# Chunk widths of a fused FFT and MLP kernel: 376, 368, 384, 368, eight times 512 and 432 columns in place of the widths of the frequency classes

## The chip, the cores and the metric

The kernel runs on one core of one Trainium2 chip. The metric is the device time of one execution in microseconds (us). Before the change the median of three runs is 850.53 us (849.95 to 851.07). The engines are named as in the profile: PE is TensorE (PEld its weight loads), DVE is VectorE, ACT is ScalarE, POOL is GpSimd, SP is SyncE, which issues most of the DMAs.

## The reference

```python
X = np.fft.fft(x, axis=1)                # x: (4, 3008, 256)
X = np.fft.fft(X, axis=2)
x = X.real.astype(np.float32).reshape(12032, 256)
h = x @ w_in                             # w_in: (256, 2048)
g = h * (1.0 / (1.0 + np.exp(-h)))       # silu
return (g @ w_out).astype(np.float32)    # w_out: (2048, 256)
```

A two-dimensional FFT of four batches, of which only the real part is kept, is followed by an MLP with a silu between its two products. All of it is in float32.

## The kernel before, in words

**Frequencies and classes.** The sequence is transformed for 1506 frequencies per batch, and each stands for itself and for its mirror. They come in four classes (k = 0 to 3) of 376, 378, 376 and 376 frequencies (`CLASS`, L40), so the four batches have 16 classes (c = 4b + k). `operand(c)` folds the input with sums and differences on DVE, ACT and POOL, `transform(c)` (L339) multiplies the folded rows by cosine and sine tables on PE into two PSUM tiles `po` of the tag `pq`, and `spread(c)` (L384) brings the result into SBUF. The FFT over the 256 features is not done on the data: it is multiplied into `w_in` at the start, which gives `abh` and `abl`.

**Columns and chunks.** The frequencies of all batches stand behind one another as 6024 columns. The MLP works on chunks of columns: `CHUNKS` (L42) has their widths and `STARTS` their first columns. Before the change the first four chunks are the four classes of batch 0, then come eight chunks of 512 and one of 422. A chunk has three SBUF tiles, made by `chunk(j)` (L378): `uv` with the high parts (`uvh`) and the remainders (`uvl`) of the transform's two halves, and `ub`, one row of it repeated on 128 partitions. Each has three buffers.

**Spread.** `spread(c, po)` cuts the class at the chunk borders into `parts` (L390). For each part ACT copies the high halves (L414), and DVE subtracts them from the source to get the remainders (L426). The row for `ub` is read out by a DMA on SP that repeats it on 128 partitions (L421). For k = 1 the source is PSUM, so ACT first copies the row into a tile `row` (L418), one for each part, and the high halves take one copy for each of the two tiles. For the other k the source is the SBUF tile `wide`, and its row is read from there. `row` has the tag `half` of the pool `fold_p`, which has three buffers; the tag is shared with the `wf` tiles in which blocks of the weights are put together, with `q`, and with half of the output tiles `o`.

**Steps.** A step is a chunk j and a block f of 128 of the 2048 hidden features: 13 chunks of 16 steps. `first(c, f)` (L443) has six matmuls (L449 to L451: high and low parts of weights and data) into two `pq` tiles. `act` (L459) makes `p` with `ub` on DVE (L463), then `h` as p + q and p - q for a frequency and its mirror (L464, L465). ACT applies silu (L480) and copies the rounded `g` high part (L483). `rest` (L488) makes the remainder of `g` on DVE (L495), a step later. `second(c, f)` (L497) has twelve matmuls (L512, L513, L519) into four accumulators. It runs three steps behind `first` (`LAG`), and at the end of a chunk ACT copies the accumulators (L528) and SP writes them out (L529). So PE has 18 matmuls a step, each as wide as the chunk. PSUM has four `pq` tiles, so `first` of one step waits until DVE has read the tiles of two turns ago.

**Order.** The order is written out by hand in the loop at L838, and every engine takes its work in that order. In the loop `first` of a step stands ahead of `second` of the step three before. `turns` (L784) says in which step a class is transformed: class 1 in step 11 of chunk 0, class 2 in step 12 of chunk 1, class 3 in step 12 of chunk 2, class 4 in step 3 of chunk 3, and so on. For class 1 `spread` runs inside `act` of its step, between `h` and the silu (`between`, L469). `clear_wo` puts blocks 6 and 7 of w_out into two `half` buffers in step 10 of chunk 0, and `low_wo` gives them back in step 12.

Of the kernel before, what the change touches and what calls it, by code (L numbers as in the profile page):

```python
# [38 lines left out]
NT = B * NC  # L39
CLASS = ((0, 376), (376, 378), (754, 376), (1130, 376))  # L40
CH = 512
CHUNKS = [n for _, n in CLASS] + [CH] * 8 + [422]  # L42
STARTS = [sum(CHUNKS[:j]) for j in range(len(CHUNKS))]
LAST = len(CHUNKS) - 1
LAG = 3
# [5 lines left out]
def fft_mlp(ctx, tc, x1, x2, x2_first, w_in, w_out, te_f, te_r, to_f, to_r, tz_r, t2_f, t2_r, t2f, rot1, rot2, dft, minus_eye, out):  # L51
# [326 lines left out]
    def chunk(j):  # L378
        if j not in chunks:
            uv = cp.tile([128, 2, 2, 512], F32R, tag="uv", name="uv")  # L380
            chunks[j] = uv[:, 0], uv[:, 1], cp.tile([128, 512], F32, tag="ub", name="ub"), CHUNKS[j], STARTS[j]
        return chunks[j]

    def spread(c, po):  # L384
# [4 lines left out]
        parts = []  # L389
        for j, (at, m) in enumerate(zip(STARTS, CHUNKS)):  # L390
            lo, hi = max(o, at), min(o + n, at + m)
# [381 lines left out]

    steps = [(j, f) for j in range(len(CHUNKS)) for f in range(NF)]
    plan = {}
# [238 lines left out]
```

## Time and profile before

| | |
|---|---|
| median of 3 runs | 850.53 us (849.95 to 851.07) |
| the profiled execution | 850.67 us |
| its span, from the first to the last instruction | 848.9 us |
| instructions in the span | 11020 |
| ACT, share of the span busy | 60% |
| DMA, mean over the span | 61 GB/s |

The span is 1.8 us shorter than the time of its execution. PE's granted clock is 1.00 in all forty slices of the span. Matmuls overlap in the engine, so a matmul's own duration is longer than the distance from its start to the next one's start; the distance is what PE's work takes. Where a row shows several instructions merged, its second number runs from the first start to the last end. A bracket at the end of a row is the engine's idle time ahead of it and what ended it.

### The profile page before, as it was taken

The numbers are of one execution on the slowest core, as the hardware profiler recorded it, in microseconds if no ns is written. First come the engines' busy times: TensorE is split into PE (matmuls) and PEld (weight loads), VectorE is DVE, ScalarE is ACT, GpSimd is POOL, SyncE is SP. The second block draws the span as 40 slices with busy tenths as digits, with TensorE's granted clock in tenths as the row PEclk, the third lists the DMA queues.
The fourth block names the chain that finished last, engine by engine and source line by source line (L and its number), as shares of the span: only waits on it lengthen the run. The fifth ranks groups of instructions, "written<-read, shape, count | busy, mean of one in ns | idle before, by whom it ended". The sixth has DMA issues, their size and how long they took to land.

```text
span 848.9 us, 11020 instructions
## 1 busy us (share of the span) xinstructions
PE 840.8 (99%) x4066; PEld 739.0 (87%) x4066; DVE 715.6 (84%) x1076; ACT 511.4 (60%) x650; POOL 166.3 (20%) x239
## 2 busy tenths in 40 slices
PE   8999999999999999999999999999999999999998
PEld 5799999999998888888888888888888888888997
DVE  5899999999898888998779988999787788777774
ACT  5767756556665565567566656467555655655554
POOL 4657550304040211304104000311000000000000
PEclk9999999999999999999999999999999999999999
DMA  9755454164250616116205201621020120120101
GB/s 319 275 141 73 107 103 73 21 93 63 9 138 0 109 51 94 17 9 149 10 1 148 8 3 51 107 10 50 0 10 1 50 10 0 51 10 0 50 1 42
DMA packets 24471, 52.12 MB, mean 61 GB/s; under 512 B 3633, under 2 KB 9265, under 8 KB 24417
## 3 DMA queue, kind: packets, MB, share of 16 engines
q1 hardware_dynamic: 20176, 38.21, 21.4%
q0 software_dynamic: 4240, 13.21, 8.6%
q8 instruction: 32, 0.52, 0.2%
q14 instruction: 23, 0.18, 0.1%
HBM read 36.17 MB, written 12.34 MB: 57 GB/s over the span
## 4 chain that ended last, share of the span: by engine, by line
PE 96%; DMA 2%; DVE 0%; ACT 0%; SPq 0%; issue 0%; ACTq 0%
PE acc L512 20%; PE acc L519 20%; PE acc L513 20%; PE pq L449 10%; PE pq L451 10%; PE pq L450 10%; PE pq L354 3%; DMA win<-in_w_in_dram 2%; PE pq L351 1%; PE acc L510 1%; PE pq L348 1%; ACT wf L82 0%; PE pq L682 0%; PE pw L589 0%; DVE wf L86 0%; SPq L78 0%
## 5 line engine op out<-in xcount | busy, mean ns | idle before, releaser
L480 ACT ACTIVATE h<-h 128x1024 f32<-128x1024 f32 (+4 forms) x208 | 202.6, 974 | 273.7 <-DVE h L465 271.2
L512 PE MATMUL acc<-g,woh 128*128 128x512 f32 (+3 forms) x824 | 305.7, 371 | 0.0
L513 PE MATMUL acc<-g,wol 128*128 128x512 f32 (+3 forms) x824 | 304.7, 370 | 0.0
L495 DVE TENSOR_TENSOR g<-h,g 128x1024 fp32r<-128x1024 f32 (+4 forms) x208 | 240.3, 1156 | 14.8 <-ACT g L483 14.6
L519 PE MATMUL acc<-g,woh 128*128 128x512 f32 (+3 forms) x824 | 211.3, 370 | 0.0
L483 ACT ACTIVATE g<-h 128x1024 fp32r<-128x1024 f32 (+4 forms) x208 | 202.5, 973 | 6.8 <-PE acc L513 0.5
L463 DVE SCALAR_TENSOR_TENSOR p<-ub,a,pq 128x512 f32<-128x512 f32 (+3 forms) x208 | 144.4, 694 | 67.9 <-PE pq L451 64.4
L512 PEld LDWEIGHTS acc<-g,woh 128*128 128x128 f32 x824 | 154.8, 188 | 21.0 <-ACT o L528 0.2
L513 PEld LDWEIGHTS acc<-g,wol 128*128 128x128 f32 x824 | 154.8, 188 | 20.2
L519 PEld LDWEIGHTS acc<-g,woh 128*128 128x128 f32 x824 | 152.1, 188 | 20.3
L449 PE MATMUL pq<-uv,abh 128*128 128x512 f32 (+3 forms) x416 | 156.9, 377 | 0.0
L451 PE MATMUL pq<-uv,abl 128*128 128x512 f32 (+3 forms) x416 | 154.1, 370 | 0.0
L450 PE MATMUL pq<-uv,abh 128*128 128x512 f32 (+3 forms) x416 | 153.9, 370 | 0.0
L464 DVE TENSOR_TENSOR h<-p,pq 128x512 f32<-128x512 f32 (+3 forms) x208 | 132.5, 637 | 21.7
L465 DVE TENSOR_TENSOR h<-p,pq 128x512 f32<-128x512 f32 (+3 forms) x208 | 131.1, 630 | 0.0
L449 PEld LDWEIGHTS pq<-uv,abh 128*128 128x128 f32 x416 | 78.3, 188 | 10.6 <-issue 0.2
L451 PEld LDWEIGHTS pq<-uv,abl 128*128 128x128 f32 x416 | 78.1, 188 | 10.2
L450 PEld LDWEIGHTS pq<-uv,abh 128*128 128x128 f32 x416 | 78.2, 188 | 10.1
L150 POOL DMA_DIRECT2D raw<-in_x_dram x22 | 19.1, 882 | 217.5 <-DMA raw<-in_x_dram 215.4
L234 POOL TENSOR_TENSOR ri<-ri,raw 128x256 f32<-128x256 f32 x24 | 22.8, 966 | 144.3 <-ACT ri L229 144.1
L528 ACT ACTIVATE o<-acc 128x512 f32<-128x512 f32 (+3 forms) x52 | 27.7, 556 | 14.4 <-PE acc L519 12.3
L218 POOL TENSOR_TENSOR raw<-raw 128x512 f32<-128x512 f32 x12 | 16.7, 1395 | 16.2 <-DMA raw<-in_x_dram 16.2
(140 smaller groups left out, 467.6 us busy)
## 6 DMA issues: line engine op xcount, KB each, us to landing
raw<-in_x_dram SPq DMA_DIRECT2D x22, 512.0 KB, 8.2
raw<-in_x_dram POOLq DMA_DIRECT2D x20, 512.0 KB, 7.8
out_dram<-o SPq DMA_DIRECT2D x32, 256.0 KB, 2.2
win<-in_w_in_dram SPq DMA_DIRECT2D x8, 512.0 KB, 8.8
wo<-in_w_out_dram SPq DMA_DIRECT2D x8, 512.0 KB, 9.6
out_dram<-o SPq DMA_DIRECT2D x12, 188.0 KB, 4.2
ub<-wide SPq DMA_DIRECT2D x6, 188.0 KB, 8.7
x_t<-in_x_first_dram SPq DMA_DIRECT2D x2, 512.0 KB, 9.8
```

The costliest lines, as they stand in the source:

```text
L449: nc.tensor.matmul(po, abh[:, i, fs], uvh[:, i, :n], start=True, stop=False)
L450: nc.tensor.matmul(po, abh[:, i, fs], uvl[:, i, :n], start=False, stop=False)
L451: nc.tensor.matmul(po, abl[:, i, fs], uvh[:, i, :n], start=False, stop=True)
L463: stt(p[:, :n], ub[:, :n], a128[f // 2][:, f % 2:f % 2 + 1], pq[0][:, :n], op0=ALU.mult, op1=ALU.add)
L464: tt(h[:, 0, :n], p[:, :n], pq[1][:, :n], op=ALU.add)
L465: tt(h[:, 1, :n], p[:, :n], pq[1][:, :n], op=ALU.subtract)
L480: nc.scalar.activation(h[:, sg, :n], h[:, sg, :n], AF.Silu)
L483: nc.scalar.activation(gh[:, sg, :n], h[:, sg, :n], AF.Copy)
L495: tt(gl[:, sg, :n], g[:, sg, :n], gh[:, sg, :n].bitcast(F32), op=ALU.subtract)
L512: nc.tensor.matmul(po, wo[0][f // 2][:, f % 2, es], gh[:, sg, :n], start=f == 0, stop=False)
L513: nc.tensor.matmul(po, wo[1][f // 2][:, f % 2, es], gh[:, sg, :n], start=False, stop=False)
L519: nc.tensor.matmul(accs[c][i][:, :n], wo[0][f // 2][:, f % 2, es], gl[:, sg, :n], start=False, stop=f == NF - 1)
```

## The change

One line changes. The widths of the first four chunks are no longer those of the classes, and the last chunk is 432 wide instead of 422. The sum is 6024 as before.

```diff
 CLASS = ((0, 376), (376, 378), (754, 376), (1130, 376))
 CH = 512
-CHUNKS = [n for _, n in CLASS] + [CH] * 8 + [422]
+CHUNKS = [376, 368, 384, 368] + [CH] * 8 + [432]
 STARTS = [sum(CHUNKS[:j]) for j in range(len(CHUNKS))]
 LAST = len(CHUNKS) - 1
```

The chunks now start at columns 0, 376, 744, 1128, 1496 and then every 512. Class 1 (columns 376 to 754) reaches into chunk 1 with 368 columns and into chunk 2 with 10; class 2 into chunk 2 with 374 and into chunk 3 with 2; class 3 into chunk 3 with 366 and into chunk 4 with 10. The classes of the other batches have as many parts as before, with borders ten columns further on. So `spread` issues three broadcasts more on SP, five instructions more on ACT and four more on DVE. PE has as many matmuls as before.

On ACT this is step 11 of chunk 0, from the end of step 10 (L483) over the spread of class 1 to the silu and the rounding of step 11. A line's bracket names the semaphores that the instruction waits for (DMAHW and a digit are the lanes of SP's DMAs, DMASW those of POOL's).

```order
 L483 ACTIVATE g<-h 128x2x376 [waits PE_49,Activation_49]
-L414 ACTIVATE uv<-pq_759 128x378 [waits PE_49]
-L414 ACTIVATE uv<-pq_760 128x378 [waits PE_49]
-L418 ACTIVATE row<-pq_760 1x378 [waits Pool_49]
+L414 ACTIVATE uv<-pq_759 128x368 [waits PE_49]
+L414 ACTIVATE uv<-pq_760 128x368 [waits PE_49]
+L414 ACTIVATE uv<-pq_759 128x10 [waits DMASW4_49,DMASW5_49,DMASW3_49,DMASW6_49,DMASW2_49,DMASW7_49,DMASW1_49,DMASW0_49]
+L414 ACTIVATE uv<-pq_760 128x10
+L418 ACTIVATE row<-pq_760 1x368 [waits Pool_49]
+L418 ACTIVATE row<-pq_760 1x10 [waits DMAHW6_49,Activation_49]
 L480 ACTIVATE h<-h 128x2x376 [waits DVE_49]
 L483 ACTIVATE g<-h 128x2x376 [waits Activation_49]
```

Two copies of ten columns and a second row copy have come in between the copies of the spread and the silu. The second row copy waits for a lane of SP's DMAs.

On DVE it is the same place, from the last `h` of step 11 (L465) to the remainder of `g` of step 10 (L495).

```order
 L465 TENSOR_TENSOR h<-p,pq_740 128x376
-L426 TENSOR_TENSOR uv<-pq_759,uv 128x378 [waits Activation_49]
-L426 TENSOR_TENSOR uv<-pq_760,uv 128x378 [waits PE_49,Activation_49]
+L426 TENSOR_TENSOR uv<-pq_759,uv 128x368 [waits PE_49,Activation_49]
+L426 TENSOR_TENSOR uv<-pq_760,uv 128x368 [waits PE_49,Activation_49]
+L426 TENSOR_TENSOR uv<-pq_759,uv 128x10 [waits DMASW7_49,DMASW0_49]
+L426 TENSOR_TENSOR uv<-pq_760,uv 128x10
 L495 TENSOR_TENSOR g<-h,g 128x2x376 [waits Pool_49]
```

Two remainders of ten columns have come in ahead of L495. The second wide remainder waits for ACT up to its last instruction of the spread, which was the only row copy before and is the second one now.

On SP this is the changed program there, from a load of w_out over the two broadcasts of class 1 to the next loads of x. A DMA waits until the lane that it takes has been left by its last user, and signals on that lane when it has landed.

```order
L78 DMA wo<-in_w_out_dram 128x2x1024 [waits DMAHW5_49,DMAHW1_49,DVE_49]
L421 DMA ub<-row 128x1x368 [waits DMAHW6_49,Activation_49]
L421 DMA ub<-row 128x1x10 [waits DMAHW7_49,Activation_49]
L145 DMA raw<-in_x_dram 128x1024 [waits DMAHW0_49,DMASW0_49,Pool_49]
L145 DMA raw<-in_x_dram 128x1024 [waits DMASW1_49,Pool_49]
```

The first broadcast takes lane 6 and the second, which is new, lane 7.

On PE this is `first` of step 13 of chunk 0, into the two PSUM tiles that the transform of class 1 had filled (pq_759 and pq_760; their buffers are pq_839 and pq_840 there before, pq_848 and pq_849 now).

```order
-L449 MATMUL pq_839<-uv,abh 128x376 [waits DVE_49]
-L450 MATMUL pq_839<-uv,abh 128x376
-L451 MATMUL pq_839<-uv,abl 128x376
-L449 MATMUL pq_840<-uv,abh 128x376 [waits DVE_49]
-L450 MATMUL pq_840<-uv,abh 128x376
-L451 MATMUL pq_840<-uv,abl 128x376
+L449 MATMUL pq_848<-uv,abh 128x376 [waits DVE_49,PE_49]
+L450 MATMUL pq_848<-uv,abh 128x376
+L451 MATMUL pq_848<-uv,abl 128x376
+L449 MATMUL pq_849<-uv,abh 128x376 [waits DVE_49,PE_49,Activation_49]
+L450 MATMUL pq_849<-uv,abh 128x376
+L451 MATMUL pq_849<-uv,abl 128x376
```

The matmuls stand where they stood; the first of each tile waits for DVE, which before meant the two wide remainders and now means the two of ten columns behind them, and the second tile also for ACT's last read of it, the second row copy.

## Rows read from the trace of the kernel before

**Rows 1.** The page, part 1: busy us, share of the span, instructions.

```profile
PE 840.8 (99%) x4066; PEld 739.0 (87%) x4066; DVE 715.6 (84%) x1076; ACT 511.4 (60%) x650; POOL 166.3 (20%) x239
```

**Rows 2.** The chain that ended last, in order of time: start us, us, what.

```profile
97.06 0.69 PE acc L519 x4
...
118.91 0.69 PE acc L519 x4
...
142.82 0.69 PE acc L519 x4
...
170.90 0.69 PE acc L519 x4
...
278.13 0.91 PE acc L519 x4
...
318.93 0.91 PE acc L519 x4
...
799.12 0.77 PE acc L519 x4
...
837.40 0.77 PE acc L519 x4
```

**Rows 3.** The waits: who waited for whom, us in total, times, longest.

```profile
PEld acc L512 <- ACT o L528: 0.2, 1, 0.2
```

**Rows 4.** ACT in order of time: start us, us, instruction [idle before].

```profile
66.39 0.49 ACT L414 ACTIVATE uv<-pq 128x378 fp32r<-128x378 f32 x1 [1.38 <-PE pq L354]
66.78 0.46 ACT L418 ACTIVATE row<-pq 1x378 f32<-1x378 f32 x1
67.14 0.81 ACT L480 ACTIVATE h<-h 128x752 f32<-128x752 f32 x1
```

**Rows 5.** SP's queue in order of time, 55 to 85 us.

```profile
67.26 0.52 SPq L421 DMA_DIRECT2D ub<-row  x1
80.90 2.88 SPq L145 DMA_DIRECT2D raw<-in_x_dram  x2
```

**Rows 6.** DMA issues by size: KB each, median us from issue to landing.

```profile
ub<-row SPq DMA_DIRECT2D x1, 189.0 KB, 8.7
...
ub<-wide SPq DMA_DIRECT2D x1, 135.0 KB, 7.0
...
ub<-row SPq DMA_DIRECT2D x1, 68.0 KB, 4.6
```

**Rows 7.** DVE in order of time, the spread of class 1.

```profile
67.27 0.55 DVE L426 TENSOR_TENSOR uv<-pq,uv 128x378 fp32r<-128x378 f32 x1 [1.42 <-ACT row L418]
67.74 1.21 DVE L495 TENSOR_TENSOR g<-h,g 128x752 fp32r<-128x752 f32 x1
```

**Rows 8.** PE in order of time, `first` of step 13 of chunk 0.

```profile
69.32 0.34 PE L449 MATMUL pq<-uv,abh 128*128 128x376 f32 x1
```

**Rows 9.** Groups by form, small copies and differences: busy us, mean ns, idle.

```profile
L292 ACT ACTIVATE sm<-sm 128x4 f32<-128x4 f32 x1 | 0.2, 184 | 0.0
...
L414 ACT ACTIVATE uv<-wide 128x60 fp32r<-128x60 f32 x1 | 0.3, 256 | 0.9 <-DVE wide L406 0.9
...
L313 DVE TENSOR_TENSOR xf<-sm 64x1 f32<-64x1 f32 x4 | 0.6, 153 | 0.1
...
L426 DVE TENSOR_TENSOR uv<-wide,uv 128x60 fp32r<-128x60 f32 x1 | 0.2, 215 | 0.0
```

**Rows 10.** DVE and PE in order of time, first steps of chunk 1.

```profile
83.91 0.54 DVE L465 TENSOR_TENSOR h<-p,pq 128x378 f32<-128x378 f32 x1
...
85.44 0.33 PE L449 MATMUL pq<-uv,abh 128*128 128x378 f32 x1
```

**Rows 11.** PE in order of time, 0 to 32 us.

```profile
1.78 4.43 PE L671 MATMUL pq<-wof 128*128 128x256 f32 x10 [1.78 <-POOL wof L652]
...
10.41 5.45 PE L589 MATMUL pw<-wf,once 128*128 128x256 f32 x24 [1.56 <-DVE wf L86]
...
18.14 1.89 PE L671 MATMUL pq<-wof 128*128 128x256 f32 x8
```

## The prediction, made before the result was known

> **What bounds the kernel now.** I read the page's busy times first: PE is busy for 99% of the span [rows 1], so what counts is what one matmul takes and where PE has to wait. Then the chain that ended last, for the pace of a step. A step issues 18 matmuls (six of `first`, twelve of `second`), and the last four of them (L519) recur in the chain once a step. From the first and the last of seven steps with 378 columns a step takes (118.91 - 97.06)/7 = 3.121 us; with 376 it is 3.120, with 512 it is 4.080, with 422 it is 3.480 [rows 2]. Per matmul that is 173.4, 173.3, 226.7 and 193.3 ns, or 416, 416, 544 and 464 cycles at 2.4 GHz. All four equal the columns rounded up to a multiple of 16, plus 32: 384 + 32, 384 + 32, 512 + 32, 432 + 32. PE keeps this pace without waiting: once the steps run, the longest wait that the view of waits puts before PE is 0.2 us [rows 3].
>
> **What the new sizes give.** Chunks 1 and 3 come down to 368 columns. 368 is a multiple of 16, so by the pattern a matmul takes 400 cycles, 166.7 ns, 6.67 ns less. Each chunk has 16 x 18 = 288 matmuls, so 2 x 288 x 6.67 ns = 3.84 us go. Chunk 2 (384) and the last (432) stay on the 416 and 464 cycles that they already pay for [rows 2]. All of this lies on PE, which sets the end. If the pattern were not one of 16, the nearest rows say what is left: the line between 376 and 422 has (193.3 - 173.3)/46 = 0.43 ns a column, and as the columns only move between chunks, the gain would be near 0. So the bounds are 0 and 3.84 us, and I take 3.84, since four sizes fit it to a cycle.
>
> The Trainium skill ("TensorE: Matmul & The Clock Gate", section "Back-to-back issue gap") has a rule against this part: the isolated gap is N/2.4 ns plus a fixed 2.5, so linear in the columns. For 512 that estimate is 215.8 ns, and the trace has 226.7; 376 and 378 would differ by 0.8 ns, and the trace has them equal. By that rule this gain would be nothing; it is the third rival below.
>
> **What the split of class 1 costs.** Class 1 is written at step 11 of chunk 0. Its 378 columns now go to chunk 1 (368) and chunk 2 (10), so ACT copies four pieces instead of two, and there are two `row` tiles and two broadcasts. In before, ACT's second piece starts at 66.39 us, when the transform ends, the row copy at 66.78, and the silu of step 11 at 67.14 [rows 4]. SP issues the broadcast at 67.26 [rows 5], and it lands 8.7 us later [rows 6]. Nobody waits for that landing, since chunk 1 starts four steps on.
>
> In the changed order somebody does. The second row copy waits for DMAHW6. On SP that lane is the one which the first broadcast takes: a DMA waits for its lane's last user and then signals on it. The reason is the tag `half` with its three buffers: at step 11 two of them hold the w_out blocks 6 and 7 (cleared at step 10, given back at step 12), so both rows get the third, and the second may be written only when the first broadcast has been read out. ACT takes its work in order, so the silu of step 11 and all behind it stand; so does the second broadcast on SP, and the loads behind that, which were not issued before 80.9 us in any case. DVE's second remainder (L426) waited for the row copy already [rows 7]; now the row copy that it waits for is the second one. Behind it on DVE stand the two 10-column remainders, `rest` of step 10 and everything of step 12. PE's `first` of step 13 takes the PSUM tiles of the transform, and these come free with the two 10-column remainders.
>
> The sum in time of day:
> - Two 10-column copies come ahead of the first row copy. Nearest rows: 184 ns for 4 columns, 256 for 60 [rows 9]. Consecutive copies overlap by 0.1 us (0.49 us long, 0.39 apart [rows 4]), so each costs 0.1 to 0.25 us; I take 0.3 for both with their semaphores. The broadcast is issued at 67.55.
> - It carries 184 KB. Between 135 KB in 7.0 us and 189 KB in 8.7 [rows 6] that is 8.55 us: it lands at 76.1.
> - The second row copy, 0.18: 76.3. DVE's 368-column remainder, 0.47 from its start to the next [rows 7]: 76.8. The 10-column one, 0.15 to 0.22 by its nearest rows [rows 9]: 77.0.
> - PE, which began `first` of step 13 at 69.32 [rows 8], begins it at 77.0: **7.7 us** of standing.
>
> DVE takes up `rest` of step 10 at 77.15 instead of 67.74 [rows 7], 9.4 us late. It is nearly saturated there and catches up little before chunk 1. Its tightest meeting with PE behind this place is in step 0 of chunk 1: `h` is done at 83.91 + 0.54 = 84.45, and the matmul that needs its tile starts at 85.44 [rows 10], a slack of 1.0. So through DVE alone PE loses at least 9.4 - 1.0 = 8.4 us in all.
>
> **The clock.** The granted clock stands at 1.00 (2.4 GHz) throughout, and from the first projection on PE never stood longer than 1.56 us [rows 11]. The only matmuls that follow a long idle stretch are the first ten: they take 4.43 us, against 1.89 for eight of the same later [rows 11]. That is 0.42 us apart against 0.216, so the lower level of 1.2 GHz, though the view prints 1.00 there. At the upper level ten would take 1.89 + 2 x 0.216 = 2.32, so the restart cost 2.1 us. No row shows how long an idle stretch lowers the clock, so the bounds are 0 and twice this, 4.2. I take 2.1, the row of a restart. PE then loses 7.7 + 2.1 = 9.8 us, which is over the 8.4 that DVE asks for, so DVE adds nothing.
>
> The Trainium skill (same page, section "HAM oscillation — how this bites in real kernels") says that PE gaps of some microseconds send the clock back to half rate, and that the work behind the gap starts cold. By that rule the 2.1 us belong in the sum, as I have put them.
>
> **The rest at nothing.** Classes 2 and 3 also split (374 + 2, 366 + 10), with one copy on ACT, one remainder on DVE and one broadcast each. Their row lies in `wide`, so no `row` buffer is shared. The extra 0.2 us on each engine [rows 9] lie beside PE's steps, as the buffers of `pq` let DVE run a step behind; uncovered they would cost 0.4 each. The last output has ten more columns: under 0.05.
>
> **Sum.** 9.8 - 3.84 = +6.0 us. The profiled execution took 850.67 with a span of 848.9, so 856.7; against the median of 850.53 it is 856.5.
>
> **Rivals.**
> 1. The clock holds through the stand. For it: no row here shows it falling. Against it: the only long idle stretch ended at the lower level. Then DVE's 8.4 us decide: 8.4 - 3.84 = +4.6, 855.1.
> 2. The other side: the second row copy hardly waits, because the first broadcast lands soon. For it: a broadcast of 68 KB landed in 4.6 us [rows 6]. Against it: the very broadcast, only 10 columns wider, took 8.7. If it lands after L us, DVE is late by L + 0.85 and PE by L - 0.15, so the change pays below L = 4.0 us; with nothing left of the wait it gives 850.53 - 3.84 + 0.1 = 846.8.
> 3. Matmuls of 368 columns take as long as the line between the sizes says, and the columns only move. The stand is left alone: 850.53 + 9.8 = 860.3. Against it: 376 and 378 columns have one and the same time.
> 4. The change does less than it says on the bad side: DVE or ACT find another order of waits, and half of the stand is hidden, with no fall of the clock: 850.5, no change.
>
> **How the numbers follow.** Forecast 0.70 (856.5), rival 1 0.12, rival 3 0.08, rival 2 0.06, rival 4 0.04. The forecast's own range comes from the landing (7.0 to 9.0 us instead of 8.55, -1.5 and +0.5) and the clock (0 to 4.2 instead of 2.1): with both it is about 854 to 859. That takes in rival 1, and leaves out rivals 2, 3 and 4 with 0.18: 854.0 to 859.0. A measurement of this kernel can tell 0.2% (1.7 us) from no change. Faster by more than that: rival 2, 0.06; within it: rival 4, 0.04; slower: 0.90.
>
> **What the changed profile would show.** ACT's second row copy (1 x 10) stands for about 8.5 us, released by the DMA ub<-row; DVE's L426 stands until it is done, near 76.3 us; PE has one hole of 7 to 8 us near 69 to 77 us, and its matmuls right behind the hole are about 0.35 us apart instead of 0.17. The granted clock shows a stretch at half. Steps in chunks 1 and 3 take 3.00 us, those in chunk 2 3.12, those in the last chunk 3.48. No hole near 70 us, or 3.12 us for a step with 368 columns, would make the prediction wrong.

## The result, and the profile after

| | before | changed |
|---|---|---|
| median, us | 850.24 (849.85 to 851.07, 4 runs) | 856.25 (856.12 to 856.38, 4 runs) |
| ratio to before | | 1.0069, 95% interval 1.0052 to 1.0087 |
| profiled span, us | 848.9 | 854.6 |
| mean granted clock | 1.00 | 0.996 |

The change costs 6.0 us. The page's busy times hardly move against [rows 1], and that is the first thing to see: the loss is time in which PE does nothing, at one place. In the forty slices of 21 us it shows in the fourth (64 to 85 us), where PE's busy share has the digit 6 and the clock the digit 8; before, both were 9.

```profile
PE 840.0 (98%) x4066; PEld 737.1 (86%) x4066; DVE 717.0 (84%) x1080; ACT 511.5 (60%) x655; POOL 166.6 (19%) x239
...
PE   8996999999999999999999999999999999999998
...
PEclk9998999999999999999999999999999999999999
```

The view of waits over the whole span (who, its tile and line, for whom; us in total, times, longest) names the whole chain of that place:

```profile
DVE uv L426 <- ACT row L418: 9.1, 3, 8.6
ACT row L418 <- DMA ub<-row: 8.5, 1, 8.5
...
PE pq L449 <- DVE uv L426: 7.3, 1, 7.3
```

A broadcast holds up a copy on ACT, the copy a subtraction on DVE, and the subtraction a matmul on PE. DVE's 9.1 us are those of three waits, of which the one at this place has 8.6. Each link can be followed in order of time (start us, us, instruction, idle before). This is ACT, to be held against [rows 4]:

```profile
66.28 0.45 ACT L418 ACTIVATE row<-pq 1x368 f32<-1x368 f32 x1
75.26 0.17 ACT L418 ACTIVATE row<-pq 1x10 f32<-1x10 f32 x1 [8.53 <-DMA ub<-row]
75.34 0.81 ACT L480 ACTIVATE h<-h 128x752 f32<-128x752 f32 x1
```

Before, the silu (L480) followed the one row copy by 0.36 us. Now a second row copy, of ten columns, stands between them and waits 8.53 us for the first broadcast. That broadcast stands in the view of DMA issues (KB each, median us to landing), to be held against [rows 6]; the second row is the ten columns' own:

```profile
ub<-row SPq DMA_DIRECT2D x1, 184.0 KB, 8.4
ub<-row SPq DMA_DIRECT2D x1, 5.0 KB, 2.3
```

Next come DVE, to be held against [rows 7], and PE, against [rows 8]:

```profile
66.37 0.54 DVE L426 TENSOR_TENSOR uv<-pq,uv 128x368 fp32r<-128x368 f32 x1 [1.58 <-ACT uv L414]
...
75.46 0.69 DVE L426 TENSOR_TENSOR uv<-pq,uv 128x368 fp32r<-128x368 f32 x3 [8.55 <-ACT row L418]
76.07 0.93 DVE L495 TENSOR_TENSOR g<-h,g 128x752 fp32r<-128x752 f32 x1
```

```profile
68.02 0.86 PE L519 MATMUL acc<-g,woh 128*128 128x376 f32 x4
76.23 0.65 PE L449 MATMUL pq<-uv,abh 128*128 128x376 f32 x1 [7.35 <-DVE uv L426]
...
76.99 0.52 PE L451 MATMUL pq<-uv,abl 128*128 128x376 f32 x1
77.30 0.52 PE L449 MATMUL pq<-uv,abh 128*128 128x376 f32 x1
...
81.47 0.34 PE L449 MATMUL pq<-uv,abh 128*128 128x376 f32 x1
81.64 0.33 PE L450 MATMUL pq<-uv,abh 128*128 128x376 f32 x1
```

PE stands 7.35 us. Behind the hole its matmuls are 0.31 us apart and last 0.52; from 81 us on they are 0.17 apart again. That is the clock, as the table by stretches says (stretch, length; busy us and instructions of PE, PEld, DVE, ACT, POOL; granted clock; DMA share; GB/s):

```profile
66.00:70.00 4.00, 2.88 (x17) 2.56 (x15) 0.54 (x1) 0.73 (x4) 2.09 (x5) 1.00 0.59 41
70.00:78.00 8.00, 1.77 (x6) 1.80 (x7) 2.43 (x6) 2.71 (x5) 0.00 (x0) 0.75 0.47 16
78.00:81.00 3.00, 3.00 (x12) 3.00 (x11) 3.00 (x6) 2.66 (x5) 0.91 (x1) 0.53 0.02 5
81.00:84.00 3.00, 3.00 (x19) 3.00 (x18) 2.90 (x5) 1.88 (x4) 3.00 (x3) 1.00 0.00 0
```

In the third row PE is busy for all of its 3 us and issues 12 matmuls where 19 fit into the fourth: a granted clock of 0.53 on average, which is the lower level (1.2 GHz) up to about 81 us. Narrower stretches show where it changed: 1.00 up to 73 us and 0.50 from 74 us on, while PE still stands, and 1.00 again from 81.2 us. A busy PE is no sign of a full clock.

Last comes the pace of the steps. These are rows of the chain, the first and the last of seven equal steps with 368 columns, of eight with 384 and of ten with 432, against [rows 2]:

```profile
99.45 0.67 PE acc L519 x4
...
120.45 0.67 PE acc L519 x4
...
152.98 0.69 PE acc L519 x4
...
177.94 0.69 PE acc L519 x4
...
804.43 0.79 PE acc L519 x4
...
839.68 0.78 PE acc L519 x4
```

These are 3.000, 3.120 and 3.525 us a step, over 18 matmuls 400, 416 and 470 cycles at 2.4 GHz. The first two are as forecast; 432 columns were to take 464.

From the start of one step to that of the next, in both traces, the 5.7 us between the spans come apart as follows:

| Place | changed minus before, us |
|---|---|
| ahead of step 0 | -0.61 |
| step 12 of chunk 0, which ends with the hole (10.77 for 3.25) | +7.52 |
| step 13, at half clock (5.24 for 3.12) | +2.12 |
| chunk 1 (368 columns) | -1.86 |
| chunk 2 (384) | -0.13 |
| chunk 3 (368) | -1.65 |
| first steps of chunk 4, which still hold matmuls of chunk 3 | -0.24 |
| chunks 5 to 11 | 0.00 |
| last chunk (432) | +0.76 |
| behind the last step | -0.18 |

The 0.61 us ahead of step 0 lie in the work on the weights, which the change does not touch, and they differ from one profiled execution to the next: against the same trace of before, the kernels of the experiments below have 0.20 to 0.81 there. Chunk 2 has -0.24 in its first three steps, which still hold matmuls of chunk 1, and +0.11 in the fourth, where it waits.

### The profile page after: what moved, and what is told of

Its sections match the earlier page's. It is cut to its first block, busy times and chain, and to the rows that moved or that the text cites. A ratio compares the mean times of both kernels' runs of the same rounds, so it can differ in the third digit from the quotient of the medians.

```text
span 854.6 us, 11041 instructions
## 1 busy us (share of the span) xinstructions
PE 840.0 (98%) x4066; PEld 737.1 (86%) x4066; DVE 717.0 (84%) x1080; ACT 511.5 (60%) x655; POOL 166.6 (19%) x239
## 4 chain that ended last, share of the span: by engine, by line
PE 95%; DMA 3%; ACT 0%; DVE 0%; issue 0%; SPq 0%; ACTq 0%
PE acc L512 20%; PE acc L513 20%; PE acc L519 20%; PE pq L449 10%; PE pq L450 10%; PE pq L451 10%; PE pq L354 3%; DMA win<-in_w_in_dram 2%; DMA ub<-row 1%; PE pq L351 1%; PE acc L510 1%; PE pq L348 1%; ACT wf L82 0%; PE pq L682 0%; PE pw L589 0%
## 5 line engine op out<-in xcount | busy, mean ns | idle before, releaser
L480 ACT ACTIVATE h<-h 128x1024 f32<-128x1024 f32 (+5 forms) x208 | 202.5, 974 | 272.9 <-DVE h L465 270.3
L512 PE MATMUL acc<-g,woh 128*128 128x512 f32 (+4 forms) x824 | 305.1, 370 | 0.0
L513 PE MATMUL acc<-g,wol 128*128 128x512 f32 (+4 forms) x824 | 305.1, 370 | 0.0
L495 DVE TENSOR_TENSOR g<-h,g 128x1024 fp32r<-128x1024 f32 (+5 forms) x208 | 242.1, 1164 | 14.5 <-ACT g L483 14.2
L519 PE MATMUL acc<-g,woh 128*128 128x512 f32 (+4 forms) x824 | 210.5, 369 | 0.0
L483 ACT ACTIVATE g<-h 128x1024 fp32r<-128x1024 f32 (+5 forms) x208 | 202.5, 973 | 6.8 <-PE acc L513 0.5
L463 DVE SCALAR_TENSOR_TENSOR p<-ub,a,pq 128x512 f32<-128x512 f32 (+4 forms) x208 | 144.4, 694 | 64.6 <-PE pq L451 60.9
L449 PE MATMUL pq<-uv,abh 128*128 128x512 f32 (+4 forms) x416 | 157.1, 378 | 7.3 <-DVE uv L426 7.3
L451 PE MATMUL pq<-uv,abl 128*128 128x512 f32 (+4 forms) x416 | 154.0, 370 | 0.0
L450 PE MATMUL pq<-uv,abh 128*128 128x512 f32 (+4 forms) x416 | 154.0, 370 | 0.0
L464 DVE TENSOR_TENSOR h<-p,pq 128x512 f32<-128x512 f32 (+4 forms) x208 | 132.5, 637 | 22.8 <-DVE p L463 1.4
L465 DVE TENSOR_TENSOR h<-p,pq 128x512 f32<-128x512 f32 (+4 forms) x208 | 131.1, 630 | 0.0
L528 ACT ACTIVATE o<-acc 128x512 f32<-128x512 f32 (+4 forms) x52 | 27.8, 556 | 13.8 <-PE acc L519 11.7
```

Source lines behind the costliest of these rows:

```text
L449: nc.tensor.matmul(po, abh[:, i, fs], uvh[:, i, :n], start=True, stop=False)
L450: nc.tensor.matmul(po, abh[:, i, fs], uvl[:, i, :n], start=False, stop=False)
L451: nc.tensor.matmul(po, abl[:, i, fs], uvh[:, i, :n], start=False, stop=True)
L463: stt(p[:, :n], ub[:, :n], a128[f // 2][:, f % 2:f % 2 + 1], pq[0][:, :n], op0=ALU.mult, op1=ALU.add)
L464: tt(h[:, 0, :n], p[:, :n], pq[1][:, :n], op=ALU.add)
L465: tt(h[:, 1, :n], p[:, :n], pq[1][:, :n], op=ALU.subtract)
```

## The experiments

The theory: the two `row` tiles of class 1 share one buffer, so the second copy waits for the first broadcast; this alone, with a restart of the clock behind it, costs all of the time, and the widths by themselves gain. The rivals are: the widths or the reach into two chunks cost something too; the clock holds or costs more; and DVE's backlog, not the hole, sets what PE loses. The first four kernels share a before of 850.1 us (849.5 to 851.2, 16 runs), the last two one of 850.24 (13 runs).

### One row tile for the whole class

The changed kernel, but the row of class 1 is copied once into one tile, and both broadcasts read slices of it. The edit does the same to the rows of classes 5, 9 and 13, which are cut in two in the kernel before and in the changed one alike.

```diff
+        if k == 1:
+            whole = fold_p.tile([1, 512], F32, tag="half", name="row", bufs=3)[:, :n]
+            nc.scalar.activation(whole, po[1][0:1, :n], AF.Copy)
         for _, _, ub, src in parts:
-            if k == 1:
-                row = fold_p.tile([1, 512], F32, tag="half", name="row", bufs=3)[:, :src.stop - src.start]
-                nc.scalar.activation(row, po[1][0:1, src], AF.Copy)
-            else:
-                row = wide[0:1, 1, src]
+            row = whole[:, src] if k == 1 else wide[0:1, 1, src]
```

> The changed kernel with one row tile for all 378 columns of a k = 1 class, copied once; the two broadcasts read slices of it. The 10-column copies, their waits on POOL's DMAs and the two broadcasts stay. Theory (the stand comes from the shared buffer of the two row tiles, 7.5 us, and the clock's fall behind it, 2.1): both go, PE does not stand near 69 us, and the time is 856.25 - 9.6 = 846.6, some 3.6 below before. Rival (the stand comes from the split itself: the 10-column copies and their waits, or a second broadcast on SP): the time stays within 1 us of 856.25.

Measured: 847.39 us (847.07 to 847.64, 6 runs), ratio 0.9969 (0.9958 to 0.9981). ACT goes from the row copy to the silu at once, and the stretch in which the changed kernel's PE was busy for 1.77 of 8 us is full again:

```profile
66.56 0.46 ACT L417 ACTIVATE row<-pq 1x378 f32<-1x378 f32 x1
66.92 0.82 ACT L479 ACTIVATE h<-h 128x752 f32<-128x752 f32 x1
```

```profile
70.00:78.00 8.00, 8.00 (x49) 8.00 (x48) 7.79 (x12) 6.40 (x11) 6.00 (x5) 1.00 0.53 19
```

So the shared buffer costs 856.25 - 847.39 = 8.9 us (8.7 if each kernel is held against the before of its own series), and everything else in the change, the reach into two chunks included, gains 850.1 - 847.39 = 2.7. That is less than the 3.6 expected, as the widths give less. The rows of classes 5, 9 and 13 have no part in it: of the eight row copies in the changed kernel only the ten-column one of class 1 waits for a DMA, and from chunk 3 on the changed kernel and this one take the same time. So a second row tile as such costs nothing. That the other two buffers are taken at class 1 is read from the program; no run gave the second row a buffer of its own. What the widths give comes out as in the table above: -1.32 in chunk 1, -1.65 in chunk 3, +0.76 in the last. Chunk 1 gains less than chunk 3 because of one step, the fourth, which takes 3.55 us instead of 3.00 (3.32 for 3.12 before). There PE waits for ACT's `o`, and its weight load does too:

```profile
PE acc L511 <- ACT o L527: 0.2, 1, 0.2
```

```profile
PEld acc L511 <- ACT o L527: 0.5, 1, 0.5
```

### Two row tiles, and nothing else

The kernel before with its old chunk sizes; only the row of class 1 is copied in two tiles, 368 and 10 columns, with a broadcast each.

```diff
-        for _, _, ub, src in parts:
+        pieces_of_row = [(ub, src) for _, _, ub, src in parts]
+        if c == 1:
+            (ub, src), = pieces_of_row
+            pieces_of_row = [(ub[:, :368], slice(0, 368)), (ub[:, 368:], slice(368, n))]
+        for ub, src in pieces_of_row:
```

> The kernel before, its chunks unchanged; only the row of class 1 is copied in two tiles of 368 and 10 columns, with a broadcast each. Theory (the shared buffer alone makes the loss): ACT's second row copy waits about 8.5 us for the first broadcast. The first PSUM tile of step 13 comes free early here, so PE does three matmuls and then stands from 69.8 to about 76.4, 6.6 us; with 2.1 for the clock that is 8.7 and the time 850.24 + 8.7 = 858.9. Rival (the widths make the loss): within 1 us of 850.24.

Measured: 858.57 us (858.3 to 859.56, 4 runs), ratio 1.0103 (1.0089 to 1.0117), 8.5 us above before. The wait is the same one:

```profile
66.58 0.45 ACT L422 ACTIVATE row<-pq 1x368 f32<-1x368 f32 x1
75.55 0.17 ACT L422 ACTIVATE row<-pq 1x10 f32<-1x10 f32 x1 [8.51 <-DMA ub<-row]
```

With the previous run this settles the place from both sides: one row tile takes the stand away from the changed kernel, and two put it into the kernel before. Here PE gets some matmuls further before it stands, and the half clock follows as in the changed kernel (the table by stretches; this profiled execution, at 859.56 us, is the longest of the four):

```profile
70.00:78.00 8.00, 1.65 (x5) 1.65 (x6) 2.15 (x4) 2.42 (x5) 0.00 (x0) 0.61 0.50 17
78.00:82.00 4.00, 4.00 (x14) 4.00 (x14) 3.90 (x8) 3.19 (x5) 1.76 (x2) 0.50 0.02 4
```

### The short row first

The changed kernel, but class 1 writes its ten columns' row and broadcast first, the 368 after them.

```diff
-        for _, _, ub, src in parts:
+        for _, _, ub, src in parts[::-1] if c == 1 else parts:
```

> The changed kernel with class 1's two rows in the other order: the 10-column row and its broadcast first, then the 368-column row in the same buffer. Theory (the cost follows the landing time L of the first broadcast, PE late by about L - 0.15, and the clock holds through a stand as short as those of the start): a broadcast of 5 KB lands in 2.3 us, so PE stands about 1.2 us near 69 us, DVE is 3.0 us late and PE 2.1 in all; the time is 846.6 + 2.1 = 848.7, faster than before. Rival (any second row tile costs a wait of 8 to 9 us whatever its size): about 856.

Measured: 849.84 us (849.33 to 850.33, 10 runs), ratio 0.9996 (0.9987 to 1.0005); span 848.2. The buffer is still shared, but what the second copy waits for is now 5 KB, and it waits 2.44 us instead of 8.53:

```profile
66.50 0.15 ACT L418 ACTIVATE row<-pq 1x10 f32<-1x10 f32 x1
69.10 0.47 ACT L418 ACTIVATE row<-pq 1x368 f32<-1x368 f32 x1 [2.44 <-DMA ub<-row]
```

The price follows how long the first broadcast takes: so it is the wait, not the second copy or the second broadcast. The time is 1.1 us above the 848.7 that was expected. Of the 2.45 us that it lies above the version with one tile, 1.44 are at the hole, and most of the rest (0.34 + 0.53) comes at steps 18 and 19 (counted through, 16 to a chunk: steps 2 and 3 of chunk 1). These are the waits of PE from 60 to 100 us, the hole first, and then those of its weight loads (PEld):

```profile
PE pq L449 <- DVE uv L426: 1.3, 1, 1.3
PE acc L512 <- ACT o L528: 0.7, 1, 0.7
```

```profile
PEld acc L512 <- ACT o L528: 1.0, 1, 1.0
PEld pq L449 <- DVE h L465: 0.4, 1, 0.4
```

The longest one behind the hole is the wait of [rows 3], which was 0.2 us in the kernel before: `second` of a new chunk needs the accumulators that ACT empties (L528), ACT does this behind the silu, and the silu comes behind DVE's `h`. DVE and ACT have no slack at all at that meeting, so what DVE is late and does not catch up by then, PE loses there.

### PE kept busy through the stand

The changed kernel with 40 more matmuls ahead of `first` of step 13, which multiply by a tile of zeros and so add zero to an accumulator. They fill the hole, and ACT's second row copy waits 8.63 us, as against 8.53. Further edits, left out below, name the tile and have POOL set it to zero at the start.

```diff
+        if n == 13:
+            for _ in range(40):
+                nc.tensor.matmul(accs[0][0][:112, :376], nil, chunks[0][0][:, 0, :376], start=False, stop=False)
```

> The changed kernel with 40 more matmuls ahead of the first matmul of step 13, which add products with zero to an accumulator that is in use; at 173 ns each they fill 6.9 us of the 7.5 us stand. The wait itself is unchanged. Theory (half-rate matmuls behind the stand cost 2.1 us, but DVE is late by 8.9 us and asks for 8.0 of PE, 0.5 more than the stand): the clock shows no fall, steps 13 and 14 take about 3.1 us each, and the time is 856.25 - 2.1 + 0.5 = 854.6. Rival (the clock's loss is hidden, as DVE's backlog decides anyway): 856.2. Second rival (the backlog asks for nothing): 854.1.

Measured: 855.73 us (855.62 to 855.97, 4 runs), ratio 1.0068 (1.0053 to 1.0084); 0.5 below the changed kernel, whose runs reach from 856.12 to 856.38. The ratios of the two to their own befores hardly differ, but the two traces have the same 0.5 us between them from step 0 to the end. It is neither the 854.6 that was expected nor the 856.2 of the rival. PE now reaches the place without a fall of the clock:

```profile
68.49 7.10 PE L845 MATMUL acc<-uv,before_xf 128*112 128x376 f32 x40
76.11 0.41 PE L449 MATMUL pq<-uv,abh 128*128 128x376 f32 x1 [0.52 <-DVE uv L426]
```

```profile
78.00:81.00 3.00, 3.00 (x19) 3.00 (x18) 3.00 (x6) 2.67 (x5) 1.03 (x1) 1.00 0.00 0
```

In the stretch in which the changed kernel issued 12 matmuls at 0.53, this one issues 19 at 1.00, and step 13 is 2.05 us shorter. But the total falls by 0.5 only: step 18 takes 0.35 more than in the changed kernel and step 19 takes 1.06 more, at these waits of PE's weight loads:

```profile
PEld acc L512 <- ACT o L528: 1.0, 1, 1.0
PEld pq L449 <- DVE h L465: 0.4, 1, 0.4
```

They are those of the previous experiment; in the changed kernel PE has no wait from 60 to 100 us but the hole. So the fall of the clock costs 2.1 us where it happens, but some 1.4 of it (0.35 + 1.06) DVE's and ACT's backlog would take five and six steps later in any case. The hole and the backlog are not added; the later of the two decides. This kernel stands 855.73 - 847.39 = 8.3 us above the one without a stand. Since PE waits for ACT at step 19 here, I take this as what the backlog asks by itself; no run has the backlog without a hole or zeros in its place.

### A sweep of widths

The version with one row tile, with other chunk sizes and, for the order of work to fit them, the last four classes transformed at other steps (that edit, and the one for the row, are left out below).

```diff
-CHUNKS = [376, 368, 384, 368] + [CH] * 8 + [432]
+CHUNKS = [376, 368, 384, 368, 512, 496, 480, 464, 448, 440, 432, 416, 400, 440]
```

> The kernel with one row tile, cut into 14 chunks of 376, 368, 384, 368, 512, 496, 480, 464, 448, 440, 432, 416, 400 and 440 columns, with the last four classes transformed some steps later to suit: a ruler for what a step takes at each width, not a candidate. Theory of the prediction (columns rounded up to a multiple of 16, plus 32 cycles): 528, 512, 496, 480, 480, 464, 448 and 432 cycles a matmul from 496 down to 400, so steps of 3.96, 3.84, 3.72, 3.60, 3.60, 3.48, 3.36 and 3.24 us. Rival (432 took 470 cycles in the changed kernel, so odd multiples of 16 pay some 6 cycles more where they are wide): 3.96 + 0.045 for 496, 3.72 + 0.045 for 464, 3.53 for 432 and 3.24 + 0.045 for 400, the others as above.

Measured: 856.43 us in one run; it has a chunk more, so its time says nothing beside the others. Its chain does: first and last of six equal steps with 496 columns, four with 464, and ten each with 440, 416 and 400.

```profile
324.73 0.89 PE acc L518 x4
...
348.85 0.89 PE acc L518 x4
...
451.74 0.83 PE acc L518 x4
...
466.78 0.83 PE acc L518 x4
...
579.76 0.80 PE acc L518 x4
...
615.76 0.80 PE acc L518 x4
...
697.99 0.75 PE acc L518 x4
...
731.89 0.75 PE acc L518 x4
...
753.75 0.72 PE acc L518 x4
...
786.15 0.72 PE acc L518 x4
```

So 496 columns take (348.85 - 324.73)/6 = 4.02 us a step, and so on. The table has the cycles of a matmul for all widths that the traces show; 480 and 448 come from steps of the same trace:

| columns | 368 | 376 | 378 | 384 | 400 | 416 | 422 | 432 | 440 | 448 | 464 | 480 | 496 | 512 |
|---|---|---|---|---|---|---|---|---|---|---|---|---|---|---|
| cycles | 400 | 416 | 416 | 416 | 432 | 452 | 464 | 470 | 480 | 486 | 501 | 520 | 536 | 544 |
| over the columns | 32 | 40 | 38 | 32 | 32 | 36 | 42 | 38 | 40 | 38 | 37 | 40 | 40 | 32 |

Both the theory (the next multiple of 16, plus 32) and a line through all sizes miss. So does the rival on record, which raised 400 by 6 cycles and left 416, 448 and 480 at the theory's values. 368, 384, 400 and 512 pay 32 cycles over their columns, every other size in the table 36 to 42, multiples of 16 among them. The theory's values hold at 400 (432) and at 440 (480), but not at 416, 432, 448, 464, 480 and 496, where they lie 4 to 8 cycles too low. What sets these apart is open: no run tried what differs between them other than the width.

### Two last chunks of 480 and 464

The version with one row tile, in which the last 944 columns are cut as 480 + 464 instead of 512 + 432.

```diff
-CHUNKS = [376, 368, 384, 368] + [CH] * 8 + [432]
+CHUNKS = [376, 368, 384, 368] + [CH] * 7 + [480, 464]
```

> The kernel with one row tile, and seven chunks of 512, one of 480 and one of 464 in place of eight of 512 and one of 432. By the prediction's rule the cycles are 7 x 544 + 512 + 496 against 8 x 544 + 470 as measured, 6 less a matmul: 288 x 6 / 2.4 GHz = 0.7 us less, 847.4 - 0.7 = 846.7. If 464 pays like 432, the same as with one row tile, 847.4.

Measured: 848.11 us (847.45 to 848.73, 9 runs), ratio 0.9977 (0.9967 to 0.9987): 0.7 above the one with 512 + 432 (0.6 with each held against the before of its own series, and the two intervals overlap), where a gain or no difference was expected. The table explains it: 520 + 501 = 1021 cycles against 544 + 470 = 1014, so 7 cycles x 288 matmuls / 2.4 GHz = 0.8 us. This kernel's own trace has 520 and 501 cycles too, and 0.66 us more in the last two chunks than the one with 512 + 432. Of the kernels run, the one with one row tile and the chunk sizes of the change has the lowest median: 847.39 us, 2.7 below the kernel before in the runs beside it, and 8.9 below the changed one.

## Why the prediction was right

**The stand: right, nearly to its size.** 7.7 us were forecast from a broadcast of 8.55 us; it took 8.4, ACT waited 8.53, PE stood 7.35, and step 12 grew by 7.5. The reason, one buffer for two tiles, is shown by the two experiments on the row: taken out of the change it gives back 8.9 us, put alone into the kernel before it costs 8.5.

**The clock: right in what it is, and its 2.1 us are found in step 13 (+2.12).** It was priced from a restart at the head of the trace [rows 11], with bounds of 0 and 4.2. By the prediction's floor a clock that holds would give back 9.8 - 8.4 = 1.4 us of them; it gave back only 0.5, since the waits at steps 18 and 19 (0.35 + 1.06 us) take the place of most of it. Rival 1 gave 855.1 for this case; 855.73 was measured.

**The floor that DVE asks: mis-sized at both ends.** "A slack of 1.0" at step 0 of chunk 1 was read as the tightest meeting. The tightest is the wait of [rows 3], at step 3, with a slack of nothing: a wait that is there already, be it 0.2 us, marks a meeting where every further delay counts in full. Against that DVE was late by less than the 9.4 forecast: it takes up `rest` of step 10 at 76.07 instead of 67.74, 8.3 later, or 8.9 with the 0.6 by which this execution began earlier. With no slack, the 8.9 less what was caught up by then (0.6, as the difference has it) come to the 8.3 measured with the hole filled, beside the 8.4 of the prediction. That these two agree is luck: the two errors have opposite signs. Rival 2's break-even falls with it. With a 5 KB broadcast of 2.3 us ahead, the change came out at no change (0.9996), where a break-even of 4.0 us promised a gain of 1.7; 0.76 of the difference is the last chunk, and most of the rest is the lack of slack.

**The widths: the right sign, and a size off by 0.76 of 3.84 us.** Chunk 3 with its carry into chunk 4 gave 1.65 + 0.24 = 1.89 of the 1.92 forecast for each of the two chunks of 368. Chunk 1 gave 1.86 in the changed kernel, 0.2 of it the wait of [rows 3], which vanished there behind the stand; without the stand it gave 1.3, as its `second` has to wait for ACT. The prediction had all of the 3.84 lie on PE without a wait, and that is not so in chunk 1. The term that was mis-sized is "the last (432) stay on the ... 464 cycles that they already pay for": 432 columns take 470, and 6 cycles x 288 / 2.4 GHz = 0.72 us, measured as +0.76. The pattern was drawn from four sizes, and of ten more it fits 368, 384, 400 and 440 and misses six. A line, the third rival, fits no better: from 368 to 376 columns 16 cycles are added, from 376 to 384 none. So the net was -3.1, not -3.84.

**The sum.** 7.5 + 2.1 - 3.1 = 6.5, less 0.8 at the head and the tail of the run, gives the 5.7 between the spans; the forecast was 9.8 - 3.84 = 6.0, and the medians differ by 6.0. The agreement of 856.5 with 856.25 is better than the terms, whose errors (0.2 in the stand, 0.7 in the widths, 0.8 at the ends) partly cancel; that much of it is luck.

## What to carry to other kernels

When one piece of work is cut into two, follow the buffers before the instructions: a second tile under a shared tag waits until the first has been read out, by a DMA too, and an in-order engine makes everything behind it wait, so a ten-column copy cost 8.9 us; cutting the reader instead (one tile, two slices) kept the gain. A stall of PE and the backlog of the engines that feed it are not added: work out when each lets PE go on, take the later one, and take as slack zero wherever the trace already shows a wait, however small. And the time of a matmul at a new width is read from a run of that width, not from a pattern over a few others.

## What the runs showed of the hardware

- The cycles of a matmul over its columns are 32 at 368, 384, 400 and 512 and 36 to 42 at ten other widths, without an order found here; 512 + 432 columns are cheaper than 480 + 464 by 7 cycles.
- A broadcast of one row of 184 KB took 8.4 us from issue to landing with nothing beside it from SP, and 5 KB still took 2.3. Issued together, as in the version with one tile, the 5 KB landed 8.6 us after their issue, the 184 KB after 8.8.
- In a stand of 7.35 us the granted clock fell to 0.50 (1.2 GHz); PE then worked at that clock from 76.2 to about 81 us and lost 2.1 us by it. Forty matmuls with zeros in the hole held the clock at 1.00.
